# A fused attention and FFN kernel on one core: the room of the DMA scratch given to spare and shifted weight tiles, and the last output block stored in two halves

## Chip, cores and metric

One Trainium2 chip, one core. The metric is device time in microseconds of one launch; three runs of the kernel before gave 801.32, 802.25 and 802.22, median 802.22.

## What is computed

Linear attention with an RMS norm feeds a GELU FFN. All inputs and outputs are float32.

```python
kv = einsum('bhsd,bhse->bhde', k, v)              # 8 batches x 8 heads, seq 576, dim 64
out = einsum('bhsd,bhde->bhse', q, kv)
rms = sqrt(mean(out * out, axis=-1) + 1e-6)
x = (out / rms * g_norm)  -> (4608 tokens, 512)
h = x @ w_in                                      # (512, 2048)
y = 0.5 * h * (1 + erf(h / sqrt(2))) @ w_out      # (2048, 512)
```

## The kernel before

**Precision.** A float32 product is made from three products of halves: each operand is split into hi (rounded to float32r by ScalarE's copy) and lo (what is left, by VectorE's or GpSimd's subtraction), and hi*hi, hi*lo and lo*hi are summed in PSUM. A matmul that uses a lo operand waits for that subtraction.

**Chunks.** The 4608 tokens go in nine chunks of 512. In the loop that begins at line 1109, chunks 0 and 1 compute `layer1` (line 678, twelve matmuls of 512 columns for each of 16 blocks i) and, one block behind, `layer2` (line 705, twelve matmuls with weight tile w_out i as the moving operand). `gelu` writes gh and `rest` (line 697) gl, the lo half that layer 2 needs last.

**Fewer products.** While chunk 1 runs, the kernel makes sums of blocks of the weights, so that from chunk 2 on seven products of quarter blocks do the work of eight. Sums of w_in: `combine` (lines 416 and 433, VectorE), `high_sums` (ScalarE into a staging tile: w_in0 and w_in1, or x2 and x3) and `low_sums` (line 449). Sums of w_out: `sum_out` (line 537, six operations on GpSimd) at the blocks of `EARLY`, then `split_out` one block later (line 1033 on ScalarE, line 1034 on VectorE, twice). The results go to DRAM by SyncE (`product_out`, lines 400 and 405), from where `fetch` (line 500) brings them back into a ring of six SBUF tiles, `RING`; `used` issues the next fetch when a tile's last matmul has been issued. Eleven products don't go through the ring: they are kept in w_out4 to w_out7 (`KEPT_IN`) and in w_out8 to w_out11 and w_in13 to w_in15 (`KEPT_OUT`).

**Layout.** SBUF tiles of 2 x 512 floats a partition are laid out in the order of `PLACES`. `EXTRA` adds floats behind some of them: 64 behind a ring tile, so that a ring tile can be used at its start or 48 floats (`AWAY`) into it; 48 more behind the last ring tile, so that the kept tiles after it begin 48 floats further round than all others; and 16 behind the last kept tile.

**Chunk 2** uses `layer1_pair` for pairs j of blocks and the plain layer 2. `ahead_loads` loads k and v of a later batch, `ahead_matmuls` sums them (`sum_kv`) and projects the next chunk.

**Chunks 3 to 8** (class `Fast`) run layer 1 as `first_part` and `second_part` (line 546, 256 columns) and layer 2 as 28 ticks of twelve matmuls of 256 columns (line 1221). A tick (k, n) is product k for group n of blocks, in the order `TICKS`. `ready(i)` prepares the operand of tick i: hi by ScalarE (line 1198), lo by VectorE (line 1199). `combine(k, n)` (line 1188) adds blocks of the activations in place, which the later ticks read: that for tick 7 reads what `combine(2, 3)` leaves. In a tick the matmuls go in the order hi x wh, hi x wl, lo x wh, so its third matmul is the first that uses lo. `ready` runs `AHEAD` = 4 ticks before its tick, but tick 5 is prepared at the end of layer 1 and tick 6 with the first tick's work. `next_piece` prepares pieces of the next chunk's x between ticks (lines 361 and 366). After four ticks of a product `after` adds its PSUM bank to an earlier sum and stores a 256 x 256 block.

Each engine works through its own queue in the order of the program; SyncE's queue issues nearly all DMAs.

Of the kernel before, what the change touches and what calls it, by code (L numbers as in the profile page):

```python
# [8 lines left out]
F32 = mybir.dt.float32  # L9
# [28 lines left out]
def linear_attn_rms_gelu_ffn(  # L38
# [58 lines left out]
    RINGS = [f"w_in{i}" for i in RING]  # L97
    PLACES = [f"x{i}" for i in range(6)] + [f"w_in{i}" for i in (4, 5, 6, 7, 8, 9, 12)]
    PLACES += [f"w_out{i}" for i in (0, 1, 2, 3, 12, 13, 14, 15)]
    PLACES += RINGS + KEPT_IN + KEPT_OUT  # L100
    EXTRA = {name: 4 * LINE for name in RINGS}
    EXTRA[RINGS[-1]] += AWAY
    EXTRA[KEPT_OUT[-1]] = 4 * LINE - AWAY

# [423 lines left out]
    def keep(key):  # L528
        t = resident[key] = block_tile(KEPT_IN[key[1]], F32R)[:, :2 * DM]
# [543 lines left out]
    EARLY = (6, 8, 10, 12)  # L1073
# [35 lines left out]
    for s in range(PLAIN * NF):  # L1109
# [34 lines left out]
        else:  # L1144
# [17 lines left out]
    class Fast:  # L1162
# [44 lines left out]
        def matmuls(self, i):  # L1207
            k, n = self.ticks[i]
            name = self.BANKS[k]
            if k in (0, 2, 1) and n == 0:  # L1210
                self.bank[name] = bank(name)
            ps = self.bank[name]
            w = operand(self.c, ("out", k, n))
            slot, op = self.ops.pop(i)
            for p in range(2):
                hi, lo = (op[:, z * CH + p * HALF:z * CH + (p + 1) * HALF] for z in range(2))
                wh, wl = (w[:, p * DM + m * HALF:p * DM + (m + 1) * HALF] for m in range(2))
                for a in range(2):
                    at = slice(a * P, (a + 1) * P)
                    for m, (x, y) in enumerate(((hi, wh), (hi, wl), (lo, wh))):  # L1220
                        nc.tensor.matmul(  # L1221
                            out=ps[:, a * HALF:(a + 1) * HALF], lhsT=x[:, at], rhs=y,
                            start=(k in (0, 2, 1) and n + p + a + m == 0),
                            stop=(n == GROUPS - 1 and p == 1 and m == 2), skip_group_check=True,
                        )
            used(self.c, ("out", k, n))
            free.append(slot)

        def after(self, i):
# [6 lines left out]
            name = {0: "gh", 2: "gl", 4: "gl", 6: "gh", 1: "w", 3: "z", 5: "w"}[k]  # L1236
            if name in "zw":
                t = work.tile([P, DM], I32, name=name, bufs=2).bitcast(F32)
            else:
                t = work.tile([P, CH], F32, name=name, bufs=2)  # L1240
            s[k] = t
            if k in (0, 4):
                nc.scalar.copy(out=t, in_=ps)
            else:
                add(t, ps, s[{2: 0, 6: 0, 1: 6, 3: 0, 5: 2}[k]])
# [238 lines left out]
```

## Time and profile before

| | us |
|---|---|
| median of three runs | 802.22 |
| the profiled execution | 801.69 |
| its span | 799.9 |
| TensorE busy (matmul) | 791.7 |
| VectorE busy | 573.3 |
| ScalarE busy | 369.7 |
| GpSimd busy | 210.6 |

The span goes from the first to the last instruction of the profiled execution; about 1.8 us of its time lie around it. In the views, PE is TensorE, DVE VectorE, ACT ScalarE, POOL GpSimd, SP SyncE. A matmul's length in the timeline is modelled and overlaps the next one's, so pace is read from starts and from the chain of waits, whose pieces follow each other without overlap. L1221 is line 1221 of the kernel; tile names are given without their numbers, so w_out4 reads w_out. PEclk, the granted clock as a share of full speed, is 1.00 in all stretches shown.

### The profile page before, as it was taken

The numbers are of one execution on the slowest core, as the hardware profiler recorded it, in microseconds if no ns is written. First come the engines' busy times: TensorE is split into PE (matmuls) and PEld (weight loads), VectorE is DVE, ScalarE is ACT, GpSimd is POOL, SyncE is SP. The second block draws the span as 40 slices with busy tenths as digits, with TensorE's granted clock in tenths as the row PEclk, the third lists the DMA queues.
The fourth block names the chain that finished last, engine by engine and source line by source line (L and its number), as shares of the span: only waits on it lengthen the run. The fifth ranks groups of instructions, "written<-read, shape, count | busy, mean of one in ns | idle before, by whom it ended". The sixth has DMA issues, their size and how long they took to land.

```text
span 799.9 us, 16183 instructions
## 1 busy us (share of the span) xinstructions
PE 791.7 (99%) x6248; PEld 739.4 (92%) x6248; DVE 573.3 (72%) x1029; ACT 369.7 (46%) x702; POOL 210.6 (26%) x184
## 2 busy tenths in 40 slices
PE   9999999999999999999999999999999999999998
PEld 7688888887798889999999999999999999999997
DVE  3999857899647764779376946786579658965683
ACT  2787534454353433446154715463445343632460
POOL 1000021653333503460047002800263026201200
PEclk9999999999999999999999999999999999999999
DMA  9991317999996789999989998989898988899984
GB/s 349 406 375 53 119 28 260 359 350 375 340 357 233 244 323 359 385 353 351 386 298 340 352 358 294 357 308 309 299 327 310 331 302 317 300 316 346 336 296 167
DMA packets 90512, 245.39 MB, mean 307 GB/s; under 512 B 9028, under 2 KB 30788, under 8 KB 90436
## 3 DMA queue, kind: packets, MB, share of 16 engines
q1 hardware_dynamic: 90432, 244.35, 85.2%
q8 instruction: 50, 0.82, 0.4%
q14 instruction: 26, 0.21, 0.1%
q10 hardware_dynamic: 4, 0.00, 0.0%
HBM read 205.52 MB, written 35.13 MB: 301 GB/s over the span
## 4 chain that ended last, share of the span: by engine, by line
PE 88%; DMA 5%; DVE 4%; SPq 1%; issue 1%; ACT 0%; DVEq 0%
PE acc L1221 21%; PE acc L546 17%; PE h L546 15%; PE acc L705 12%; PE a L1221 8%; PE h L678 7%; PE a L242 3%; PE a L181 3%; DMA products_in<-w_in 2%; DMA w_in<-products_in 2%; SPq L405 1%; PE h L670 1%; PE h L790 1%; DVE w L433 1%; DVE z L416 1%
## 5 line engine op out<-in xcount | busy, mean ns | idle before, releaser
L705 PE MATMUL acc<-w_out,gh 128*128 128x512 f32 x312 | 97.8, 394 | 0.0
L229 POOL TENSOR_TENSOR ql<-q,qh 128x512 fp32r<-128x512 f32 x16 | 21.5, 1342 | 262.6 <-ACT qh L228 262.6
L678 PE MATMUL h<-x,w_in 128*128 128x512 f32 x360 | 87.3, 392 | 0.0
L1221 PE MATMUL acc<-w_in,w_out 128*128 128x256 f32 x696 | 86.1, 278 | 0.0
L1221 PEld LDWEIGHTS acc<-w_in,w_out 128*128 128x128 f32 x696 | 82.7, 188 | 0.0
L678 PEld LDWEIGHTS h<-x,w_in 128*128 128x128 f32 x360 | 67.5, 188 | 14.5 <-POOL x L332 0.2
L705 PEld LDWEIGHTS acc<-w_out,gh 128*128 128x128 f32 x312 | 57.9, 188 | 12.4
L705 PE MATMUL acc<-w_out,gl 128*128 128x512 f32 x156 | 61.5, 394 | 1.8 <-DVE gl L697 1.6
L546 PE MATMUL acc<-w_out,w_in 128*128 128x256 f32 x450 | 61.0, 280 | 0.8 <-DMA w_in<-products_in 0.6
L546 PEld LDWEIGHTS acc<-w_out,w_in 128*128 128x128 f32 x450 | 55.6, 188 | 1.4 <-ACT w_out L602 0.8
L691 ACT ACTIVATE gh<-h 128x512 fp32r<-128x512 f32 x39 | 23.2, 595 | 70.1 <-PE h L678 45.9
L546 PE MATMUL h<-w_in,w_in 128*128 128x256 f32 x402 | 52.1, 277 | 0.4 <-DMA w_in<-products_in 0.4
L546 PEld LDWEIGHTS h<-w_in,w_in 128*128 128x128 f32 x402 | 48.7, 188 | 0.7 <-issue 0.5
L546 PE MATMUL acc<-x,w_in 128*128 128x256 f32 x360 | 48.1, 278 | 0.0
L1221 PE MATMUL acc<-w_in,x 128*128 128x256 f32 x360 | 45.5, 278 | 0.0
L546 PEld LDWEIGHTS acc<-x,w_in 128*128 128x128 f32 x360 | 44.3, 188 | 0.2
L1221 PEld LDWEIGHTS acc<-w_in,x 128*128 128x128 f32 x360 | 43.2, 188 | 0.0
L546 PE MATMUL h<-x,w_in 128*128 128x256 f32 x312 | 41.5, 279 | 0.0
L537 DVE TENSOR_TENSOR gl<-acc,gh 128x256 f32<-128x256 f32 (+1 forms) x66 | 29.3, 444 | 16.9 <-ACT gh L583 13.6
L265 DVE TRANSPOSE_TENSOR_REDUCE part<-sq 128x16 f32<-128x512 f32 x33 | 23.4, 709 | 23.1 <-ACT sq L252 23.1
L546 PEld LDWEIGHTS h<-x,w_in 128*128 128x128 f32 x312 | 39.2, 189 | 0.7
L583 ACT COPY gh<-h 128x256 f32<-128x256 f32 x18 | 6.8, 376 | 68.2 <-PE h L546 68.2
(287 smaller groups left out, 1855.9 us busy)
## 6 DMA issues: line engine op xcount, KB each, us to landing
w_in<-products_in SPq DMA_DIRECT2D x172, 512.0 KB, 5.4
w_in<-products_out SPq DMA_DIRECT2D x126, 512.0 KB, 5.4
kv_main<-kv_main SPq DMA_DIRECT2D x22, 512.0 KB, 6.8
products_in<-w_in SPq DMA_DIRECT2D x40, 256.0 KB, 5.3
w_in<-w_in SPq DMA_DIRECT2D x16, 512.0 KB, 10.2
w_out<-w_out SPq DMA_DIRECT2D x16, 512.0 KB, 10.2
q<-qT SPq DMA_DIRECT2D x15, 512.0 KB, 6.7
products_out<-w_out SPq DMA_DIRECT2D x20, 256.0 KB, 4.6
```

The source lines that it names most:

```text
L181: nc.tensor.matmul(out=ps[r, n * D:(n + 1) * D], lhsT=k[:, r], rhs=v[:, r], start=(j == 0), stop=(j == NJ),)
L229: eng.tensor_tensor(out=ql, in0=q, in1=qh.bitcast(F32), op=ALU.subtract)
L242: nc.tensor.matmul(out=ps[:, a:e], lhsT=w, rhs=x[:, a:e], start=(m == 0), stop=(m == 2))
L265: nc.vector.tensor_reduce(out=self.part[:, p, :], in_=sq.rearrange("p (b d) -> p b d", d=BLK), op=ALU.add, axis=AX.X, apply_transpose=True,)
L405: eng.dma_start(out=to.rearrange("p (a n) -> p a n", a=2), in_=src.bitcast(F32))
L416: nc.vector.tensor_tensor(out=whole[a], in0=w[:, HI], in1=w[:, LO], op=ALU.add)
L537: eng.tensor_tensor(out=out, in0=x, in1=y, op=op)
L546: nc.tensor.matmul(out=out, lhsT=y, rhs=x[:, z, kb], start=first and kb + i == 0, stop=kb == 1 and i == 2, skip_group_check=True,)
L678: nc.tensor.matmul(out=h, lhsT=parts["in", i][:, w][:, p * P:(p + 1) * P], rhs=at.x[p][:, x], start=(m + p == 0), stop=(m == 2 and p == NP ...
L691: nc.scalar.activation(out=gh, in_=h, func=AF.Gelu)
L705: nc.tensor.matmul(out=ps, lhsT=x[:, ts], rhs=parts["out", i][:, w], start=(i == 0 and m == 0), stop=(m == 2 and (i == NF - 1 or (i, t) == ...
L1221: nc.tensor.matmul(out=ps[:, a * HALF:(a + 1) * HALF], lhsT=x[:, at], rhs=y, start=(k in (0, 2, 1) and n + p + a + m == 0), stop=(n == GRO ...
```

## The change

The kernel asks for 1 KB of scratch for dynamic DMAs instead of 16, which gives 15 KB a partition to SBUF tiles. There are three new tiles, s0 to s2; every ring tile and every kept tile gets 64 floats behind it, so that all tiles begin at the same residue, and the kept products lie 48 floats into their tiles. s0 and s1 are the staging tiles of `high_sums` for j = 6, s2 one of those of the last `split_out`; later all three join the tiles that `take` gives out. `EARLY` is two blocks earlier. In chunk 2, loads of k and v and their sum move one pair later. In chunk 3 the two calls of `raw_out` move from j = 1 and 3 to 2 and 5. In each of chunks 3 to 8 tick 6 is prepared at the end of layer 1, ahead of the two combines. In the last chunk products 1 and 5 accumulate their two sides in two banks, and the last four ticks run for side 0 first, which is added and stored, and then for side 1.

```diff
-    PLACES += RINGS + KEPT_IN + KEPT_OUT
-    EXTRA = {name: 4 * LINE for name in RINGS}
-    EXTRA[RINGS[-1]] += AWAY
-    EXTRA[KEPT_OUT[-1]] = 4 * LINE - AWAY
+    PLACES += SPARE + RINGS + KEPT_IN + KEPT_OUT
+    EXTRA = {name: 4 * LINE for name in RINGS + KEPT_IN + KEPT_OUT}
...
-                resident[key] = block_tile(KEPT_OUT[KEPT_KEYS.index(key[1])], F32R)
+                t = block_tile(KEPT_OUT[KEPT_KEYS.index(key[1])], F32R)
+                resident[key] = t[:, AWAY:AWAY + 2 * DM]
...
-                t = piece(block_tile(f"x{2 + second}", F32R))
+                t = piece(block_tile(SPARE[second] if j == 6 else f"x{2 + second}", F32R))
...
-        t = resident[key] = block_tile(KEPT_IN[key[1]], F32R)[:, :2 * DM]
+        t = resident[key] = block_tile(KEPT_IN[key[1]], F32R)[:, AWAY:AWAY + 2 * DM]
...
-    EARLY = (6, 8, 10, 12)
+    EARLY = (4, 6, 8, 10)
...
-                split_out(n, [f"w_in{m}" for m in ((4, 5), (6, 7), (4, 5), (6, 9))[n]])
+                split_out(n, (("w_in4", "w_in5"), ("w_in6", "w_in7"), ("w_in4", "w_in5"),
+                              (SPARE[2], "w_in9"))[n])
...
-            if i >= len(self.ticks):
+            if i >= len(self.ticks) or i in self.ops:
                 return
...
-        def matmuls(self, i):
+        def matmuls(self, i, sides=(0, 1)):
...
+            two = self.c == NCH - 1 and name == "a0"
+            if k in (0, 2, 1) and n == 0 and 0 in sides:
+                self.bank[name] = [bank(name), bank("a1")] if two else [bank(name)] * 2
...
-                for a in range(2):
+                for a in sides:
...
-        def after(self, i):
+        def after(self, i, sides=(0, 1)):
...
+            halves = [sides] if ps[0] is ps[1] else [(a,) for a in sides]
+            for part in halves:
+                cols = slice(part[0] * HALF, (part[-1] + 1) * HALF)
+                t, x = s[k][:, cols], ps[part[0]][:, cols]
+                if k in (0, 4):
+                    nc.scalar.copy(out=t, in_=x)
+                else:
+                    add(t, x, s[{2: 0, 6: 0, 1: 6, 3: 0, 5: 2}[k]][:, cols])
...
-            if c + 2 < B and at == (3, 2):
+            if c + 2 < B and at == (4, 2):
                 split_kv(c + 2, range(NP))
...
-        if c + 2 < B and (j, between) == (3, 0):
+        if c + 2 < B and (j, between) == (4, 0):
             sum_kv(c + 2, range(NP))
...
-        if c + 2 < B and j < 2:
-            for p in (2 * j, 2 * j + 1):
-                (load_main if j else load_kv)(c + 2, p)
-        if c + 2 < B and j == 1:
+        if c + 2 < B and 1 <= j < 3:
+            for p in (2 * j - 2, 2 * j - 1):
+                (load_main if j > 1 else load_kv)(c + 2, p)
+        if c + 2 < B and j == 2:
             load_tails(c + 2)
...
-    free += ["x4", "x5", "x0", "x1", "w_in12"]
+    free += ["x4", "x5", "x0", "x1", "w_in12"] + SPARE
...
-            if c == FAST and second and j in (1, 3):
-                raw_out(NJ2 - 2 + j // 2)
-                free.extend(f"w_out{n}" for n in (NF - 5 + j, NF - 4 + j))
+            if c == FAST and second and j in (2, 5):
+                raw_out(NJ2 - 2 + j // 3)
+                free.extend(f"w_out{n + 2 * (j // 3)}" for n in (NF - 4, NF - 3))
...
             if second and j % 2:
-                last = j == NJ2 - 1
                 layer.ready(TICKS.index((0, j // 2)))
+                if last:
+                    layer.ready(TICKS.index((2, j // 2 - 1)))
                 for k in (6, 2):
                     layer.combine(k, j // 2, nc.vector if last else nc.gpsimd)
...
+        if c == NCH - 1:
+            for side in range(2):
+                for i in range(len(layer.ticks) - GROUPS, len(layer.ticks)):
+                    layer.matmuls(i, (side,))
+                    layer.after(i, (side,))
...
-    nc = bacc.Bacc("TRN2", target_bir_lowering=False, num_devices=1)
+    nc = bacc.Bacc("TRN2", target_bir_lowering=False, num_devices=1,
+                   dynamic_dma_scratch_size=1024)
```

How the instructions of an engine stand before and after, at three places. A row is a line, an operation and its tiles with their numbers.

VectorE at the change from layer 1 to layer 2 of chunk 4 (L1199 and L1200 write the lo of a tick's operand, L1188 and L1189 are the combines, L366 and L365 a low block of the next chunk). Before:

```order
L537 TENSOR_TENSOR acc_4982<-acc_4982,gl 128x512
L1199 TENSOR_TENSOR w_out_5094<-x_5042,w_out_5094 128x512
L1188 TENSOR_TENSOR x_5042<-w_in_5043,x_5042 128x512
L1188 TENSOR_TENSOR x_5042<-x_5042 128x512
L1199 TENSOR_TENSOR x_5126<-w_out_4894,x_5126 128x512
L366 TENSOR_TENSOR w_out_5144<-o,w_out_5144 128x512
L1199 TENSOR_TENSOR w_in_5147<-x_5042,w_in_5147 128x512
L1199 TENSOR_TENSOR w_in_5164<-w_in_4550,w_in_5164 128x512
```

Now:

```order
L537 TENSOR_TENSOR acc_4985<-acc_4985,gl 128x512
L1200 TENSOR_TENSOR w_in_5097<-x_5045,w_in_5097 128x512
L1200 TENSOR_TENSOR s_5100<-w_in_4897,s_5100 128x512
L1189 TENSOR_TENSOR x_5045<-w_in_5046,x_5045 128x512
L1189 TENSOR_TENSOR x_5045<-x_5045 128x512
L365 TENSOR_TENSOR w_out_5147<-o,w_out_5147 128x512
L1200 TENSOR_TENSOR w_out_5150<-x_5045,w_out_5150 128x512
L1200 TENSOR_TENSOR x_5167<-w_out_4553,x_5167 128x512
```

The lo of tick 6 (x_5126 before, s_5100 now) went ahead of the two combines; all that follows the combines stands where it stood, the lo of tick 7 among it.

VectorE in chunk 1, around gl of block 13 (L697, h_2135 before, h_2148 now; L356 and L355 add blocks of the next chunk's x, L1034 is `split_out`). Before:

```order
L697 TENSOR_TENSOR gl<-h_2073,gh 128x512
L449 TENSOR_TENSOR w_in_1509<-w,w_in_1509 128x2x256
L356 TENSOR_TENSOR z<-o 128x512
L356 TENSOR_TENSOR o<-o 128x2x256
L356 TENSOR_TENSOR w<-z,o 128x512
L366 TENSOR_TENSOR w_in_2156<-o,w_in_2156 128x512
L697 TENSOR_TENSOR gl<-h_2135,gh 128x512
L1034 TENSOR_TENSOR w_in_2164<-w_in_2116,w_in_2164 128x2x256
L1034 TENSOR_TENSOR w_in_2167<-w_in_2116,w_in_2167 128x2x256
L356 TENSOR_TENSOR z<-o,w 128x512
```

Now:

```order
L697 TENSOR_TENSOR gl<-h_2094,gh 128x512
L449 TENSOR_TENSOR w_in_1512<-w,w_in_1512 128x2x256
L355 TENSOR_TENSOR z<-o 128x512
L355 TENSOR_TENSOR o<-o 128x2x256
L355 TENSOR_TENSOR w<-z,o 128x512
L365 TENSOR_TENSOR w_in_2169<-o,w_in_2169 128x512
L697 TENSOR_TENSOR gl<-h_2148,gh 128x512
L355 TENSOR_TENSOR z<-o,w 128x512
```

The last `split_out` left this place; it now stands two blocks earlier, ahead of gl of block 12, and each of the three others one place of the same kind earlier.

SyncE in layer 1 of chunk 3, from the second send of raw weights (L400) on (L500 is a fetch of the ring, L147 and L164 load k and v; they are L146 and L163 now). Before:

```order
L400 DMA w_in_3511<-w_out_1142 128x2x256
L400 DMA w_in_3513<-w_out_1228 128x2x256
L400 DMA w_in_3515<-w_out_1228 128x2x256
L147 DMA kv_main<-kv_main 128x1024
L164 DMA kv_tail<-kv_tail 128x256
L500 DMA w_in_1500<-products_in_0_2024 128x1024
L500 DMA w_in_1509<-products_in_1_2030 128x1024
L500 DMA w_in_2188<-products_in_2_1900 128x1024
```

Now:

```order
L146 DMA kv_main<-kv_main 128x1024
L163 DMA kv_tail<-kv_tail 128x256
L500 DMA w_in_1503<-products_in_0_2049 128x1024
L500 DMA w_in_1512<-products_in_1_2055 128x1024
L500 DMA w_in_2191<-products_in_2_1921 128x1024
L146 DMA kv_main<-kv_main 128x1024
L163 DMA kv_tail<-kv_tail 128x256
L500 DMA w_in_2193<-products_in_2_2051 128x1024
L500 DMA w_in_2319<-products_out_0_1447 128x1024
L500 DMA w_in_2321<-products_out_1_1602 128x1024
L400 DMA w_in_3602<-w_out_1145 128x2x256
L400 DMA w_in_3604<-w_out_1231 128x2x256
```

The three sends went from ahead of this fetch of products_in_0 to behind the first fetches of products_out.

## Rows read from the trace of the kernel before

**Rows 1.** The page, part 1: busy time, share of the span, instructions.
```profile
PE 791.7 (99%) x6248; PEld 739.4 (92%) x6248; DVE 573.3 (72%) x1029; ACT 369.7 (46%) x702; POOL 210.6 (26%) x184
```

**Rows 2.** The chain that ended last, chunk 0: start us, us, what.
```profile
46.98 2.72 PE acc L705 x12
...
53.38 2.80 PE acc L705 x12
...
94.27 2.80 PE acc L705 x12
```

**Rows 3.** The waits of PE: waited for, us in total, times, longest.
```profile
PE acc L705 <- DVE gl L697: 1.6, 1, 1.6
...
PE acc L546 <- DMA w_in<-products_in: 0.6, 1, 0.6
```

**Rows 4.** The chain, layer 2 of chunks 3 and 4.
```profile
351.37 21.86 PE acc L1221 x192
373.23 5.44 PE a L1221 x48
...
389.55 2.78 PE h L546 x24
...
434.39 22.45 PE acc L1221 x192
456.84 5.65 PE a L1221 x48
...
473.80 2.85 PE h L546 x24
```

**Rows 5.** The timeline of PE, chunk 4, ticks 5 and 6: start us, us, what.
```profile
441.13 1.52 PE L1221 MATMUL acc<-w_in,w_out 128*128 128x256 f32 x12
442.49 1.63 PE L1221 MATMUL acc<-w_in,x 128*128 128x256 f32 x12
```

**Rows 6.** The timeline of DVE at the same place.
```profile
439.99 0.69 DVE L1199 TENSOR_TENSOR w_out<-x,w_out 128x512 fp32r<-128x512 f32 x1 [1.17 <-ACT w_out L1198]
440.60 0.69 DVE L1188 TENSOR_TENSOR x<-w_in,x 128x512 f32<-128x512 f32 x1
441.32 0.69 DVE L1188 TENSOR_TENSOR x<-x 128x512 f32<-128x512 f32 x1
441.93 0.68 DVE L1199 TENSOR_TENSOR x<-w_out,x 128x512 fp32r<-128x512 f32 x1
```

**Rows 7.** The page, part 3: a DMA queue's packets, MB, share of 16 engines.
```profile
q1 hardware_dynamic: 90432, 244.35, 85.2%
```

**Rows 8.** The timeline of DVE, chunk 1, beside the fourth sum of w_out.
```profile
198.15 1.67 DVE L356 TENSOR_TENSOR o<-o 128x512 f32<-128x512 f32 x1
```

**Rows 9.** Windows: PE, PEld, DVE, ACT, POOL busy, PEclk, DMA share, GB/s.
```profile
140.00:150.00 10.00, 10.00 (x48) 8.36 (x47) 7.83 (x12) 5.09 (x10) 5.24 (x4) 1.00 1.05 361
...
190.00:200.00 10.00, 9.87 (x43) 7.76 (x42) 9.86 (x12) 4.78 (x9) 7.39 (x5) 1.00 1.06 365
...
310.00:350.00 40.00, 39.40 (x398) 38.85 (x397) 27.75 (x55) 18.26 (x36) 22.30 (x17) 1.00 1.03 388
```

**Rows 10.** The timeline of SP, chunk 3: the second send of raw weights.
```profile
330.75 1.96 SPq L400 DMA_DIRECT2D w_in<-w_out  x3
```

**Rows 11.** The chain, the fetch that follows it.
```profile
334.90 7.69 DMA w_in<-products_in
```

**Rows 12.** The timeline of ACT, chunk 4: hi of ticks 5 and 7.
```profile
439.35 0.61 ACT L1198 CAST w_out<-x 128x512 fp32r<-128x512 f32 x1
...
442.05 0.62 ACT L1198 CAST w_in<-x 128x512 fp32r<-128x512 f32 x1 [1.05 <-DVE x L1188]
```

**Rows 13.** The chain, its last piece.
```profile
796.08 0.69 DVE w L537
```

**Rows 14.** Line 537 by operation: min/median/max ns, first and last start, forms.
```profile
L537 DVE TENSOR_TENSOR h<-h,gh x18: 399/420/433, 312.9 to 757.3; 128x256 f32<-128x256 f32 x18
```

**Rows 15.** DMA from 793 us on: issues, KB each, median us to landing.
```profile
out<-w SPq DMA_DIRECT2D x1, 256.0 KB, 2.2
```

More of the change, by code (lines that the diff above doesn't have):

```diff
@@ L97, in linear_attn_rms_gelu_ffn @@
     RINGS = [f"w_in{i}" for i in RING]
+    SPARE = ["s0", "s1", "s2"]
     PLACES = [f"x{i}" for i in range(6)] + [f"w_in{i}" for i in (4, 5, 6, 7, 8, 9, 12)]
     PLACES += [f"w_out{i}" for i in (0, 1, 2, 3, 12, 13, 14, 15)]
-    PLACES += RINGS + KEPT_IN + KEPT_OUT
-    EXTRA = {name: 4 * LINE for name in RINGS}
-    EXTRA[RINGS[-1]] += AWAY
-    EXTRA[KEPT_OUT[-1]] = 4 * LINE - AWAY
+    PLACES += SPARE + RINGS + KEPT_IN + KEPT_OUT
+    EXTRA = {name: 4 * LINE for name in RINGS + KEPT_IN + KEPT_OUT}
     def block_tile(name, dtype):
@@ L1205, in linear_attn_rms_gelu_ffn @@
         BANKS = {0: "acc2", 4: "acc2", 2: "acc3", 6: "acc3", 3: "acc3", 1: "a0", 5: "a0"}
-        def matmuls(self, i):
+        def matmuls(self, i, sides=(0, 1)):
             k, n = self.ticks[i]
             name = self.BANKS[k]
-            if k in (0, 2, 1) and n == 0:
-                self.bank[name] = bank(name)
-            ps = self.bank[name]
+            two = self.c == NCH - 1 and name == "a0"
+            if k in (0, 2, 1) and n == 0 and 0 in sides:
+                self.bank[name] = [bank(name), bank("a1")] if two else [bank(name)] * 2
             w = operand(self.c, ("out", k, n))
-            slot, op = self.ops.pop(i)
+            slot, op = self.ops[i]
             for p in range(2):
@@ L1221, in matmuls @@
                         nc.tensor.matmul(
-                            out=ps[:, a * HALF:(a + 1) * HALF], lhsT=x[:, at], rhs=y,
-                            start=(k in (0, 2, 1) and n + p + a + m == 0),
+                            out=self.bank[name][a][:, a * HALF:(a + 1) * HALF],
+                            lhsT=x[:, at], rhs=y,
+                            start=(k in (0, 2, 1) and n + p + m == 0 and (two or a == 0)),
                             stop=(n == GROUPS - 1 and p == 1 and m == 2), skip_group_check=True,
                         )
-            used(self.c, ("out", k, n))
-            free.append(slot)
-        def after(self, i):
+            if 1 in sides:
+                used(self.c, ("out", k, n))
+                free.append(slot)
+                self.ops.pop(i)
+        def after(self, i, sides=(0, 1)):
             k, n = self.ticks[i]
@@ L1235, in after @@
             s = self.sums
[L1236 to L1245, printed above, removed]
+            if 0 in sides:
+                name = {0: "gh", 4: "gl", 2: "gl", 6: "gh", 1: "w", 3: "z", 5: "w"}[k]
+                if name in "zw":
+                    t = work.tile([P, DM], I32, name=name, bufs=2).bitcast(F32)
+                else:
+                    t = work.tile([P, CH], F32, name=name, bufs=2)
+                s[k] = t
+            halves = [sides] if ps[0] is ps[1] else [(a,) for a in sides]
[4 more added lines that the diff above has]
+                    nc.scalar.copy(out=t, in_=x)
+                else:
+                    add(t, x, s[{2: 0, 6: 0, 1: 6, 3: 0, 5: 2}[k]][:, cols])
+            t = s[k][:, sides[0] * HALF:(sides[-1] + 1) * HALF]
             at = {4: (0, 0), 1: (1, 1), 3: (0, 1), 5: (1, 0)}.get(k)
             if at:
-                r = self.c * CH + at[0] * HALF
-                to = out[r:r + HALF, at[1] * HALF:(at[1] + 1) * HALF]
+                r = self.c * CH + at[0] * HALF + sides[0] * P
+                to = out[r:r + len(sides) * P, at[1] * HALF:(at[1] + 1) * HALF]
                 nc.sync.dma_start(
                     out=to.rearrange("(a p) n -> p a n", p=P),
-                    in_=t.rearrange("p (a n) -> p a n", a=2),
+                    in_=t.rearrange("p (a n) -> p a n", a=len(sides)),
                 )
@@ L1425, in linear_attn_rms_gelu_ffn @@
                     layer.ready(i)
+            last = j == NJ2 - 1
             if second and j % 2:
-                last = j == NJ2 - 1
                 layer.ready(TICKS.index((0, j // 2)))
+                if last:
+                    layer.ready(TICKS.index((2, j // 2 - 1)))
                 for k in (6, 2):
@@ L1438, in linear_attn_rms_gelu_ffn @@
                 layer.combine(1, i - 9)
-            layer.matmuls(i)
-            layer.after(i)
+            if c < NCH - 1 or i < len(layer.ticks) - GROUPS:
+                layer.matmuls(i)
+                layer.after(i)
             within_layer2(c, layer, i)
+        if c == NCH - 1:
[3 more added lines that the diff above has]
+                    layer.after(i, (side,))
 def kernel(q, k, v, g_norm, moe_w_in, moe_w_out):
```

## Prediction

> **What bounds the kernel now.** I read the page first. TensorE is busy for 791.7 us, 99% of the span [rows 1]. So an edit counts only where TensorE waits, where its matmuls run slower than elsewhere, or after the last of them. The views behind that: the chain by stretches, because a stretch of equal matmul counts shows by its length where the pace is worse; the waits of TensorE; then the timelines of the engines that feed the place. Three things show.
>
> Pace of 512-column matmuls: in layer 2 of chunk 0 twelve matmuls take 2.72 us with most weight tiles and 2.80 us in the eight rows from 53.38 to 94.27 [rows 2], which are the blocks i = 4 to 11: the tiles w_out4 to w_out11, and by the code those alone begin 48 floats off the others.
>
> Waits: of the longest, 1.6 us stands before a layer-2 block of chunk 1, for VectorE's gl (line 697), and 0.6 us in layer 1 of chunk 3, for a product that the ring fetched [rows 3].
>
> Pace of 256-column matmuls: the first 192 matmuls of layer 2 take 21.86 us in chunk 3 and 22.45 in chunk 4, the next 48 take 5.44 and 5.65, and the next layer 1 begins with 2.78 and 2.85 for 24 [rows 4]. Chunk 5 repeats chunk 4's lengths. Per chunk that is 0.59 + 3 x 0.21 + 0.07 = 1.3 us, and I add an estimated 0.1 for the rest of that layer 1: 1.4 us. It begins at one place. Ticks 5 and 6 start at 441.13 and 442.49, 1.36 us apart; the first is listed with 1.52 us, the second with 1.63 [rows 5]. The third matmul of a tick is the first that needs lo (lines 1220 and 1222); two matmuls into tick 6 is 442.49 + 2 x 1.36/12 = 442.72. VectorE's lo for it (line 1199) runs from 441.93 for 0.68, to 442.61 [rows 6]. So 0.11 us from the end of lo to its matmul is too little, and after this short wait the pace stays slow for the rest of layer 2.
>
> **The change, part by part.**
>
> *Scratch.* Nothing but room is taken. The transfers are on one hardware queue, 244.35 MB [rows 7], which SyncE feeds (ScalarE issues two tiny ones). I cost it at 0; no row tells what a smaller scratch would do to an issue, so the bounds are nothing on one side, and on the other issues that take longer, of which the ring's six tiles hide some tenths of a us each and the last store hides none: 0 to +0.4. [...]
>
> *Residue of the kept tiles.* Eight blocks x 0.08 us in chunk 0: -0.64 [rows 2]. In chunk 1 the same eight stand among VectorE's waits, which can swallow the gain: 0 to -0.64, I take -0.3. In chunk 2 the odd pairs keep gh in w_in13 and w_in14, which lie at the shifted place as well, so that about four of the eight pay now: -0.3. Together -1.2, ends -0.6 and -1.6. That a tile's start sets the pace is a reading of these rows only. [...]
>
> *Sums of w_out two blocks earlier (EARLY).* Before, GpSimd's fourth sum runs beside VectorE's add_blocks from 195.8: an operation of line 356 takes 1.67 us there [rows 8], where the same shape takes 0.69 [rows 6]. VectorE works 9.86 of 10 us from 190 to 200 with GpSimd busy for 7.39, and gl of block 13 comes 1.6 us late [rows 3, 9]. After, this sum stands at block 10, so this stretch is free of it: -1.6. What is paid: all four splits now precede block 12's gl, one more than before: two operations of 128x512, which follow each other by 0.6 us as in [rows 6], so 1.2 us of VectorE, with ScalarE's two copies beside it, and the sums press on earlier operations, about one and a half of them by 1.67 - 0.69 = 0.98, so 1.5 us. VectorE has 10 - 7.83 = 2.2 us to spare from 140 to 150 [rows 9]. The remainder, 1.2 + 1.5 - 2.2 = 0.5, arrives as a wait at block 10, where the first rsqrt and scale stand ahead of gl. Four sends of 256 KB go earlier on SyncE, past the sends of w_in's products; x2 and x3 no longer wait for the staging of j = 6, since it has s0 and s1. Net -1.1; ends -1.6 (all hidden) and +4.0 (see the second rival).
>
> *Chunk 2.* The loads of k and v come one pair later, sum_kv's 40 matmuls and split_kv too. Counts stay, both have pairs of slack, and SyncE's queue in front of its last sends is as before. 0, between -0.6 (its late fetch vanishes) and +0.3.
>
> *raw_out at j = 2 and 5.* Three sends of 256 KB are issued from 330.75 ahead of the fetch of 334.90, which takes 7.69 us to land; at the same time the transfers use a share of 1.03 of the engines [rows 9 to 11]. At 388 GB/s three such sends are 0.79 MB, 2.0 us. Behind the fetch instead of ahead of it, they let it land some 2.0 us sooner, and it was 0.6 late: -0.6 [rows 3]. The later fetches then carry the 2.0 us; they have the ring's depth.
>
> *Tick 6 prepared before the combines.* VectorE's order was lo5, comb6, comb2, lo6, the next chunk's low block, lo7; now it is lo5, lo6, comb6, comb2, low block, lo7. From chunk 4's rows: lo6 takes the start 440.60, 1.33 us sooner, and is no longer late. comb6 then starts at 441.21 (0.61 later), comb2 0.72 after it (441.32 - 440.60), at 441.93 [rows 6]. ScalarE's hi7 reads what comb2 writes: it started at 442.05, 0.73 after comb2 at 441.32 [rows 6, 12], so now at 442.66. lo7 follows its hi by 0.64, as lo5 at 439.99 follows the hi of 439.35 [rows 6, 12], so it starts at 443.30 and ends 0.69 later, at 443.99. Without the wait at tick 6, tick 7 starts at 442.49 + 1.36 = 443.85 and needs lo at 444.08. That leaves 0.09 us, and 0.11 was too little at tick 6. **So the late thing is next lo7**: the same short wait, one tick on, with the same slow pace after it. Chunks 4 and 5 gain one tick of the slow pace, (5.65 - 5.44)/4 = 0.05 us each: -0.1. And chunk 3, whose lo operations were 0.6 us early because TensorE had waited in layer 1, loses that margin with the wait: it then meets the same wait at tick 7 and pays what chunk 4 pays: +1.3. Chunks 6 to 8 run at the fast pace and have no such edge. With raw_out, chunk 3 is +0.7; all of this -0.1 + 0.7 = +0.6.
>
> *Tail.* The last add takes 0.69 us on 128x512 [rows 13]; an add on 128x256 has a median of 0.42 [rows 14]: -0.27. The last store is 256 KB and lands 2.2 us after its issue [rows 15]; half of it saves half of its moving time, an estimated 0.25 us from 128 KB at the 388 GB/s of [rows 9] with a margin for its fixed part. Side 0's add and store lie beside the last 24 matmuls (2.7 us), and the halved add of k = 1 beside the 5.4 us of k = 3. -0.5, ends -0.2 and -0.7.
>
> **Sum.** -1.2 - 1.1 + 0 + 0.6 - 0.5 = -2.2 us. Against the profiled execution (801.69) that is 799.5, against the median of the runs (802.22, 0.53 above it) 800.0; I give 799.8, between them, and count the rivals from the same middle, 802.0.
>
> **The rivals.**
> *The new order is enough* (chance 0.2): lo7 is in time, tick 7 doesn't wait, and chunks 3 to 8 all run at 5.44. For it: 0.09 against 0.11 is a matter of hundredths, and the end of an operation is not exactly where its data are seen. Against: tick 6 failed with more. Time: 2 x 1.4 saved in chunks 4 and 5 and 0.6 in chunk 3, so -1.2 - 1.1 - 0.6 - 2.8 - 0.5 = -6.2, 795.8.
> *Slower: chunk 1 gets a longer wait at block 10 than it loses at block 13* (0.08). The four sends moved ahead are 1.05 MB, 2.9 us at the 361 GB/s of 140 to 150, where the transfers already use 1.05 [rows 9]. If the staging tiles of w_in's sums come free that much later, VectorE can't use its spare 2.2 us, and gl of block 10 is 1.2 + 1.5 + 2.9 = 5.6 us late: 5.6 - 1.6 = +4.0 in place of -1.1, total +2.9, 804.9. It decides from a lateness of 2.7 us (then nothing is gained over before), and can be measured from 4.3. Against it: s0 and s1 free two of these tiles.
> *The residue is not what makes 2.80* (0.1): the eight blocks keep 2.80, because their place in the work sets it and not their address. The term of 1.2 is gone, -2.2 + 1.2 = -1.0, 801.0. Against it: blocks before and after them, in the same work, take 2.72. [...]
>
> **How the numbers follow.** My own case has 0.62 and, from the ends of its terms, 797.6 to 801.6. A measurement of this kernel can tell about 0.2%, 1.6 us, from no change; 800.6 is the edge. Two thirds of my case lie below it (0.41), 0.2 within, 0.01 above. With the first rival (0.20) and a part of the third, faster has 0.63; same 0.27; slower, from the second rival and ends, 0.10. The range reaches down to the first rival and up past the third: 795.4 to 802.6; what is left out is most of the second rival and a few hundredths below.
>
> **What would show it.** Right: eight rows of 2.72 in chunk 0; no wait for gl at block 13 but one of some tenths near block 10; no wait for a fetch in layer 1 of chunk 3; in chunks 3, 4 and 5 the first 192 matmuls near 22.4 and then 5.65; a last add of 0.42 and a store of 128 KB. Wrong: 5.44 in chunks 4 and 5 (lo7 was in time); 5.44 in chunk 3 with its wait in layer 1 still there; rows of 2.80 in chunk 0 (residue); a wait of over 2.7 us in chunk 1.

## The result, and the profile after

| | us |
|---|---|
| kernel before, median of 22 runs | 800.57 (798.35 to 802.30) |
| changed kernel, median of 22 runs | 802.62 (800.78 to 807.02) |
| ratio | 1.0034, 95% interval 1.0022 to 1.0046 |

The change makes the kernel slower: by 0.34%, 2.7 us, as the ratio has it; the medians lie 2.05 us apart, and eight of the changed kernel's 22 runs are longer than 803 us. The forecast was 799.8 us, faster; the measured median lies 0.02 us above the stated range. The forecast counted from 802.0, and the 22 runs of the kernel before give 800.57, so the change itself was missed by more than the times say: 2.2 us gained were forecast, 2.05 to 2.7 were lost. The profiled execution of before (801.69) was a long one among its 22 runs; a second profile of the same kernel, below, shows why.

What was gained stands where it was looked for. The chain that ended last, chunk 0 of the changed kernel (start us, us, what), against [rows 2]:

```profile
46.97 2.72 PE acc L705 x12
...
53.36 2.72 PE acc L705 x12
...
93.61 2.72 PE acc L705 x12
```

All eight rows of 2.80 are 2.72, and chunk 0 is 0.9 us shorter. The rest of the chain, against [rows 4] and [rows 13]:

```profile
214.95 4.83 PE h L546 x42
...
311.85 2.83 PE acc L546 x24
...
353.79 22.09 PE acc L1222 x192
375.87 5.44 PE a L1222 x48
...
437.03 21.95 PE acc L1222 x192
458.99 5.44 PE a L1222 x48
...
520.49 22.41 PE acc L1222 x192
542.90 5.65 PE a L1222 x48
...
797.02 0.43 DVE w L537
```

In the kernel before, the first, second and third of these pieces start at 213.49, 308.82 and 351.37. So chunk 2 starts 1.5 us later although chunk 0 was shorter, chunk 3 starts 3.0 us later, and its layer 1 wins 0.6 back: 41.9 us instead of 42.5. Layer 2 of chunks 3 and 4 runs at 5.44, that of chunk 5 at 5.65. The last add is the short one. The loss is in chunks 1 and 2. The waits of TensorE in the changed kernel (waited for, us in total, times, longest), against [rows 3]:

```profile
PE acc L705 <- DVE gl L697: 4.8, 2, 2.6
PE h L546 <- DVE w_in L537: 1.9, 2, 1.3
```

The wait for gl has grown from 1.6 to 4.8 us, the wait for the ring's fetch is gone, and chunk 2 waits for VectorE's line 537. Windows of chunk 1 (PE, PEld, DVE, ACT, POOL busy, PEclk, DMA share, GB/s), against [rows 9]:

```profile
140.00:150.00 10.00, 10.00 (x48) 8.40 (x47) 9.26 (x14) 5.09 (x10) 5.93 (x5) 1.00 1.03 370
...
180.00:190.00 10.00, 7.43 (x33) 5.78 (x32) 9.62 (x21) 2.35 (x5) 1.39 (x2) 1.00 1.04 385
190.00:200.00 10.00, 7.72 (x34) 6.10 (x33) 9.86 (x13) 5.40 (x11) 4.29 (x3) 1.00 1.06 395
```

VectorE is busy nearly all the time, TensorE is not from 180 to 200. VectorE's timeline there shows where its time goes:

```profile
184.56 0.69 DVE L697 TENSOR_TENSOR gl<-h,gh 128x512 fp32r<-128x512 f32 x1
...
191.84 1.78 DVE L1034 TENSOR_TENSOR s<-w_in,s 128x512 fp32r<-128x512 f32 x1
193.54 1.77 DVE L1034 TENSOR_TENSOR w_in<-w_in,w_in 128x512 fp32r<-128x512 f32 x1
...
198.06 0.68 DVE L697 TENSOR_TENSOR gl<-h,gh 128x512 fp32r<-128x512 f32 x1
```

The first row is gl of block 10, the last gl of block 12. The two operations of the last `split_out`, now ahead of block 12, take 1.78 us each where 0.68 is usual. In between stands GpSimd:

```profile
191.62 1.46 POOL L365 TENSOR_TENSOR x<-o,x 128x512 fp32r<-128x512 f32 x1 [10.23 <-ACT x L360]
193.03 1.74 POOL L228 TENSOR_TENSOR ql<-q,qh 128x512 fp32r<-128x512 f32 x1
```

### The profile page after: what moved, and what is told of

Same layout as the page of the kernel before. It is cut to its first block, busy times and chain, and to the rows that moved or that the text cites. A ratio compares the mean times of both kernels' runs of the same rounds, so it can differ in the third digit from the quotient of the medians.

```text
span 800.1 us, 16160 instructions
## 1 busy us (share of the span) xinstructions
PE 788.6 (99%) x6248; PEld 738.0 (92%) x6248; DVE 577.5 (72%) x1031; ACT 369.8 (46%) x702; POOL 211.9 (26%) x184
## 4 chain that ended last, share of the span: by engine, by line
PE 88%; DVE 5%; DMA 4%; issue 1%; SPq 1%; POOL 0%; ACT 0%; DVEq 0%; POOLq 0%
PE acc L1222 21%; PE acc L546 18%; PE h L546 15%; PE acc L705 12%; PE a L1222 8%; PE h L678 7%; PE a L241 3%; PE a L180 3%; DMA products_in<-x 1%; PE h L670 1%; DMA q<-qT 1%; PE h L790 1%; SPq L405 1%; DMA kv_main<-kv_main 1%; DVE w L433 1%
## 5 line engine op out<-in xcount | busy, mean ns | idle before, releaser
L678 PEld LDWEIGHTS h<-x,w_in 128*128 128x128 f32 x360 | 67.4, 188 | 13.9 <-POOL x L331 0.2
L1222 PE MATMUL acc<-w_in,w_out 128*128 128x256 f32 x456 | 56.9, 277 | 0.0
L546 PE MATMUL h<-w_in,w_in 128*128 128x256 f32 x420 | 54.5, 278 | 1.9 <-DVE w_in L537 1.9
L1222 PEld LDWEIGHTS acc<-w_in,w_out 128*128 128x128 f32 x456 | 54.3, 188 | 0.0
L546 PEld LDWEIGHTS h<-w_in,w_in 128*128 128x128 f32 x420 | 51.0, 188 | 2.5 <-DVE w_in L537 2.5
L1222 PE MATMUL acc<-w_in,w_in 128*128 128x256 f32 x384 | 48.0, 277 | 0.0
L1222 PEld LDWEIGHTS acc<-w_in,w_in 128*128 128x128 f32 x384 | 45.7, 188 | 0.0
L1222 PE MATMUL acc<-w_in,x 128*128 128x256 f32 x336 | 42.7, 277 | 0.0
L546 PE MATMUL acc<-w_in,w_in 128*128 128x256 f32 x300 | 41.6, 278 | 0.0
L705 PEld LDWEIGHTS acc<-w_out,gl 128*128 128x128 f32 x156 | 29.3, 188 | 12.1 <-DVE gl L697 5.9
L1222 PEld LDWEIGHTS acc<-w_in,x 128*128 128x128 f32 x336 | 40.4, 188 | 0.0
L546 PEld LDWEIGHTS acc<-w_in,w_in 128*128 128x128 f32 x300 | 37.6, 188 | 0.2
```

Source lines behind the costliest of these rows:

```text
L546: nc.tensor.matmul(out=out, lhsT=y, rhs=x[:, z, kb], start=first and kb + i == 0, stop=kb == 1 and i == 2, skip_group_check=True,)
L678: nc.tensor.matmul(out=h, lhsT=parts["in", i][:, w][:, p * P:(p + 1) * P], rhs=at.x[p][:, x], start=(m + p == 0), stop=(m == 2 and p == NP ...
L705: nc.tensor.matmul(out=ps, lhsT=x[:, ts], rhs=parts["out", i][:, w], start=(i == 0 and m == 0), stop=(m == 2 and (i == NF - 1 or (i, t) == ...
L1222: nc.tensor.matmul(out=self.bank[name][a][:, a * HALF:(a + 1) * HALF], lhsT=x[:, at], rhs=y, start=(k in (0, 2, 1) and n + p + m == 0 and ...
```

## Experiments

Each run is compared with runs of the kernel before on the same chip; ratios to it are given with their 95% interval. The chips differ (the kernel before has medians from 799.25 to 800.57), so two runs are compared by their ratios. Small differences are read from the chain: where chunk 2 starts, where chunk 3 starts, and the pace of layer 2. Where chunk 2 starts is not exact either: profiles of kernels that are the same up to there differ by 0.1 to 0.6 us, in one case by 1.4. The edits of the first four runs start from the changed kernel.

**EARLY put back.**

```diff
-    EARLY = (4, 6, 8, 10)
+    EARLY = (6, 8, 10, 12)
```

(with the four places of `split_out` as before).

> The changed kernel with EARLY and the places of split_out put back as before; s0 and s1 still serve the staging of j = 6. [...] Theory B (TensorE reaches block 10 about 0.9 us sooner since the weights' residue no longer slows it, and VectorE would be late anyway): a wait of 0.7 us or more stays at block 10, and blocks 12 and 13 wait longer than before by what block 10 does not take, so that less than 2 us is gained.

Measured: 802.08 us, ratio 1.0020 (1.0010 to 1.0029); chunk 2 starts at 214.19. B's size holds, under 2 us, but its place does not: block 10 waits only 0.3 us, and the waits for gl are still 3.5 us, most of it now at block 12. The ratio is 0.14% below the changed kernel's 1.0034, 1.1 us, and the intervals overlap; chunk 2 starts 0.8 us sooner. So the earlier sums are at most a part of the loss, and something else holds VectorE ahead of block 12. VectorE in this run, the two operations of `split_out`, and GpSimd beside them:

```profile
189.63 3.47 DVE L1034 TENSOR_TENSOR w_in<-w_in,w_in 128x512 fp32r<-128x512 f32 x2
```

```profile
189.41 1.45 POOL L365 TENSOR_TENSOR x<-o,x 128x512 fp32r<-128x512 f32 x1 [10.23 <-ACT x L360]
190.82 1.74 POOL L228 TENSOR_TENSOR ql<-q,qh 128x512 fp32r<-128x512 f32 x1
192.52 3.41 POOL L537 TENSOR_TENSOR w_in<-w_out 128x512 f32<-128x512 f32 x2
```

In the kernel before, GpSimd's same three began 3.1 to 3.3 us later and met nothing of `split_out`; ScalarE's copy into x2, on which the first depends, had waited for a DMA (its timeline and GpSimd's, kernel before):

```profile
191.84 0.62 ACT L361 CAST x<-o 128x512 fp32r<-128x512 f32 x1 [2.29 <-DMA products_in<-x]
```

```profile
192.54 1.62 POOL L366 TENSOR_TENSOR x<-o,x 128x512 fp32r<-128x512 f32 x1 [12.62 <-DMA products_in<-w_in]
...
195.82 3.44 POOL L537 TENSOR_TENSOR w_in<-w_out 128x512 f32<-128x512 f32 x2
```

That DMA reads the staging tile x2, which s0 now replaces.

**Chunk 2's loads put back.**

```diff
-        if c + 2 < B and 1 <= j < 3:
-            for p in (2 * j - 2, 2 * j - 1):
-                (load_main if j > 1 else load_kv)(c + 2, p)
-        if c + 2 < B and j == 2:
+        if c + 2 < B and j < 2:
+            for p in (2 * j, 2 * j + 1):
+                (load_main if j else load_kv)(c + 2, p)
+        if c + 2 < B and j == 1:
```

(with `split_kv` at (3, 2) and `sum_kv` at (3, 0)).

> The changed kernel with chunk 2's loads of k and v at j = 0 and 1 again, and their sum and split at j = 3. Theory C (the load of q at j = 2 now stands behind two loads and the tails on SyncE, lands 7.1 us after its issue, and by ScalarE, GpSimd's low half and GpSimd's scale holds VectorE, so that TensorE waits 1.3 us at 261): the waits for VectorE's line 537 in chunk 2 fall from 1.9 us to under 0.7, chunk 2 is 1.2 to 1.6 us shorter, and the run is as much faster than the changed kernel; chunk 1 is unchanged. Rival D (the waits in chunk 2 come from chunk 1's lateness, from its sends that still fill the queue): no difference.

Measured: 801.12 us, ratio 1.0012 (1.0002 to 1.0023), 0.22% or 1.8 us below the changed kernel's; its list of waits has none for line 537 any more, chunk 1 ends as in the changed kernel (chunk 2 starts at 214.77), and chunk 2 takes 95.1 us instead of 96.9. C holds. The chain of the changed kernel had shown the way:

```profile
243.32 7.11 DMA q<-qT
...
250.46 0.63 ACT qh L227
...
251.16 1.29 POOL ql L228
...
255.59 1.30 POOL o L314
...
260.75 0.44 DVE w_in L537
```

**Both put back.**

> Both put back. [...] By B and D under 2 us faster than the changed kernel, and no faster than before.

Measured: 800.28 us, ratio 1.0002 (0.9991 to 1.0014). By the ratios this is 2.6 us below the changed kernel, and the two alone gave 1.1 and 1.8: they roughly add, to more than the 2 us that B and D allow, and EARLY's part is the smaller. The kernel is level with the one before and not faster.

**Both put back, the first combine ahead of tick 5's operand.**

```diff
-                layer.ready(TICKS.index((0, j // 2)))
                 if last:
+                    layer.combine(6, j // 2)
+                    layer.ready(TICKS.index((0, j // 2)))
+                    layer.combine(2, j // 2)
                     layer.ready(TICKS.index((2, j // 2 - 1)))
-                for k in (6, 2):
-                    layer.combine(k, j // 2, nc.vector if last else nc.gpsimd)
+                else:
+                    layer.ready(TICKS.index((0, j // 2)))
+                    for k in (6, 2):
+                        layer.combine(k, j // 2, nc.gpsimd)
```

> Both put back, and at the end of layer 1 of chunks 3 to 8 the first combine goes ahead of the operand of tick 5, the second between those of ticks 5 and 6. By the timeline of the kernel before, the first combine then runs from about 439.5, lo5 from 440.1, the second combine from 440.7, lo6 from 441.3, hi7 from 441.4 and lo7 from at most 442.5: every lo ends 0.6 us or more ahead of its matmul. If the short wait at tick 7 starts the slow pace in a part of the executions (seen in chunk 5 here, not in 3 and 4), all six chunks run at 5.44 us for 48 matmuls and this run is 0.4 to 3 us faster than the one with both put back. If the slow pace has another cause, 5.65 is seen again in some chunk.

Measured: 798.81 us, ratio 0.9987 (0.9977 to 0.9997), 1.5 us less than the run before it. Layer 2 takes 21.86 and 5.44 us in every chunk:

```profile
352.10 21.86 PE acc L1221 x192
373.96 5.44 PE a L1221 x48
...
435.12 21.86 PE acc L1221 x192
456.99 5.44 PE a L1221 x48
...
518.49 21.86 PE acc L1221 x192
540.35 5.44 PE a L1221 x48
```

The run with both put back had 5.65 in chunk 3.

This profile shows one thing more. TensorE waits 2.9 us for gl of block 12, until 196.84, and soon after it begins again its granted clock falls from 1.00 to 0.50. Windows (PE, PEld, DVE, ACT, POOL busy, PEclk, DMA share, GB/s):

```profile
195.00:196.00 1.00, 0.00 (x0) 0.00 (x0) 0.96 (x2) 0.00 (x0) 0.92 (x2) 1.00 1.04 393
...
198.00:199.00 1.00, 1.00 (x3) 0.79 (x3) 0.96 (x2) 0.87 (x2) 1.00 (x1) 0.50 1.06 260
...
202.00:203.00 1.00, 1.00 (x6) 0.83 (x5) 1.00 (x2) 0.47 (x1) 0.45 (x1) 1.00 0.27 102
```

There three matmuls take 1.28 us instead of 0.69. Block 13's gl matmuls begin 7.2 us after block 12's; in the run with only EARLY put back, where the clock stays at 1.00 after a like wait, it is 5.8 without the wait between them. So this wait cost some 1.4 us more than its length, and chunk 2 starts 0.4 to 0.6 us later here than in the runs with EARLY or both put back, which are the same up to there. Two other profiles show the fall too, after 2.4 and 2.6 us (chunk 2's loads put back, and EARLY alone, below); the changed kernel's own does not. Each run also has its mean granted clock on record. It is 0.998 or less in 49 of 75 runs of the six kernels whose longest wait for gl in the profile is 2.4 to 2.9 us, and in none of 100 runs of the kernels whose longest is 1.6 or less. Of the changed kernel's 22 runs it is so in 14, with a median of 803.5 us against 802.0 for the other eight. What makes the clock fall in one execution and not in the next stays open.

**The staging put back**, on top of that.

```diff
-                t = piece(block_tile(SPARE[second] if j == 6 else f"x{2 + second}", F32R))
+                t = piece(block_tile(f"x{2 + second}", F32R))
```

> The kernel with EARLY and chunk 2's loads put back and the combine first, and now also the staging of j = 6 in x2 and x3 again instead of s0 and s1. Theory S (in the kernel before, ScalarE's copy into x2 waited 2.3 us for the DMA that reads x2, and so GpSimd's low half of x, its low half of q and the fourth sum began 3.1 us later, at 192.5; without that wait they run beside VectorE's two operations of split_out, which then take 3.47 us instead of 1.29, and gl of block 12 comes late): the two operations take about 1.3 us again, GpSimd's low half of x begins 2 to 3 us later, the wait at block 12 falls from 3 to under 2 us, and chunk 2 begins 0.5 to 1.5 us sooner than in the run with s0 and s1. Rival R (TensorE simply comes 1.5 us sooner to a VectorE that is never idle): the waits for gl stay at 3 us or more in sum, and chunk 2 begins within 0.3 us of 213.9.

Measured: 796.34 us, ratio 0.9956 (0.9943 to 0.9970); against 0.9987 without this edit that is 0.3%, 2.5 us, and the intervals do not overlap. Chunk 2 starts at 212.39, against 214.62. Three profiles without this edit that are alike up to there have 214.01 to 214.62, three with it (two of them below) 212.26 to 212.51: 1.5 to 2.4 us. VectorE's and GpSimd's timelines, with this edit:

```profile
189.30 1.29 DVE L1034 TENSOR_TENSOR w_in<-w_in,w_in 128x512 fp32r<-128x512 f32 x2
```

```profile
191.79 1.30 POOL L365 TENSOR_TENSOR x<-o,x 128x512 fp32r<-128x512 f32 x1 [12.94 <-ACT x L360]
...
194.74 3.44 POOL L537 TENSOR_TENSOR w_in<-w_out 128x512 f32<-128x512 f32 x2
```

And without it, the run before:

```profile
189.34 3.47 DVE L1034 TENSOR_TENSOR w_in<-w_in,w_in 128x512 fp32r<-128x512 f32 x2
```

```profile
189.12 1.45 POOL L365 TENSOR_TENSOR x<-o,x 128x512 fp32r<-128x512 f32 x1 [10.23 <-ACT x L360]
```

So the edit moves GpSimd by 2.7 us, VectorE's two operations are back at 1.29 us, and TensorE's wait at block 12 falls from 2.9 to 0.4 us; 1.6 us stand at block 13 again, as in the kernel before. All five runs have a granted clock of 1.00, so what the fall of the clock cost is in the 2.5 us too. S holds; R falls. This kernel beats both.

**The fourth sum of w_out in chunk 2**, on top of that.

```diff
-    EARLY = (6, 8, 10, 12)
+    EARLY = (6, 8, 10)
-    SUMS = {1: (4,), 3: (5,), 5: (6,), 7: (7,)}
+    SUMS = {1: (4,), 2: (3,), 3: (5,), 5: (6,), 7: (7,)}
```

> The same, and the fourth sum of w_out is made in chunk 2, at j = 2, instead of at block 12 of chunk 1, its split at j = 3. By theories S and R alike, 8 us of GpSimd and two operations of VectorE leave the stretch in which VectorE is never idle: the wait at block 13 goes and the one at block 12 shrinks by the 0.5 us or so that the scale operations lose beside the sum; chunk 2 begins 1 to 2 us sooner. If chunk 2 has room, the whole is 1 to 2 us faster than the run before it; if VectorE's line 537 or a late fetch waits for it there, less.

Measured: 795.70 us, ratio 0.9959 (0.9946 to 0.9971), not to be told from the run before it. Chunk 2 starts 2.4 us sooner (209.99), and takes 1.8 us longer: line 537 is 0.9 us late once more, and a fetch 0.9. Ahead of line 537 stands GpSimd's scale at 252. The sum itself was done by then; the scale waits for VectorE's transpose (line 318), and ahead of that VectorE now has the sum's split, 1.3 us at 250.

**The residue alone**, on the kernel before: the smaller scratch, `EXTRA` and the two slices at `AWAY` of the change, nothing else.

> The kernel before, with the smaller scratch and all tiles at one residue, the kept products 48 floats into their tiles, and nothing else. If the residue makes 2.80 of 2.72, the eight rows of chunk 0 read 2.72 and chunk 0 ends 0.8 us sooner. If chunk 1 is bound by VectorE, the wait for gl grows by what TensorE gains, so that chunk 2 begins less than 0.4 us sooner than at 213.3; if not, 1.3 us sooner. In chunk 2 and 3 the wait for the fetch stays. The run is 0 to 1 us faster than the kernel before.

Measured: 798.59 us, ratio 0.9991 (0.9982 to 1.0000). Chunk 0 reads 2.72 in all rows, and chunk 2 starts at 213.06, 0.3 to 0.4 us sooner; the waits for gl grow to 2.5 us. Chunk 2 takes 95.7 us, where the two profiles of the kernel before have 95.3 and 95.5, with a wait of 0.8 us for a fetch: nothing is gained there. So VectorE swallows most of what layer 2 gains in chunk 1.

**The kernel before, a second profile.**

> The kernel before, a second profile. The slow pace after the wait at tick 6 came in both of its chunks 4 and 5 there, but after the like wait at tick 7 in only 4 of 12 chunks of the changed kernels. If it is a matter of chance, this profile has it in none or one of the two and its span is 1.4 or 2.8 us shorter than 799.9; if the old order makes it, 5.65 us stand in both again.

Measured: 799.09 us, a span of 797.2. The same instructions in the same order:

```profile
434.48 21.97 PE acc L1221 x192
456.45 5.44 PE a L1221 x48
...
517.96 21.97 PE acc L1221 x192
539.93 5.44 PE a L1221 x48
```

The short wait at tick 6 is still in the 21.97 (21.86 without it), but the slow pace isn't: tick 6 of chunk 4 takes 1.47 us here and 1.46 in the first profile, and the ticks after it 1.36 here and 1.41 to 1.42 there. Over all profiles with a short wait at tick 6 or 7, 5.65 follows it in 6 of 19 chunks; in the seven runs with the combine first, in none of 21.

Against this profile the changed kernel's 2.9 us can be followed through the chain: chunk 2 starts 1.6 us later and takes 1.4 us longer, layer 1 of chunk 3 is 0.7 us shorter, layer 2 of chunk 3 to layer 1 of chunk 6 takes 1.3 us more (the slow pace in chunk 5), and the end is 0.7 us shorter.

**EARLY alone**: the run with the staging put back, and the earlier sums with s2.

> The run with the staging put back, and EARLY at 4 to 10 again, with s2 for the last split: the earlier sums without the staging in s0 and s1. Theory A2 (one more split and one more sum ahead of block 10, where VectorE has no idle time, cost by themselves): a wait of 2 to 3 us at block 10 comes back, the wait at block 13 goes, chunk 2 begins 1 to 2 us later than 212.2, and the run is 1 to 2 us slower than with EARLY put back. Rival S2 (it was the staging alone that made the sums collide): no wait over 1 us at block 10, chunk 2 begins at 212.2 or sooner, and the run is as fast or faster.

Measured: 797.52 us, ratio 0.9965 (0.9951 to 0.9979). One wait of 2.6 us in the list, at block 10, none at 12 or 13; chunk 2 starts at 213.49, 1.1 us later than without. A2 holds in its place and at the low end of its size; the ratios alone (0.9965 and 0.9956) overlap. In this profile the granted clock falls to 0.50 after the wait, so the 1.1 us hold that too.

**The fourth sum at j = 4 of chunk 2.**

> The run with the fourth sum of w_out in chunk 2, the sum at j = 4 instead of 2, so that GpSimd's scale of the next chunk at j = 3 no longer stands behind it. If the scale behind the sum made the wait of 0.9 us for line 537 at 258, that wait goes and the gain of 2.4 us up to the start of chunk 2 is kept but for the wait for the fetch near 281 (0.9 us): chunk 3 begins near 305.5 to 306, against 307.0 and 307.6, and the run takes 794 to 795 us. If chunk 2 loses elsewhere what chunk 1 gains, it stays at 795.5 or more.

Measured: 796.67 us, ratio 0.9955 (0.9941 to 0.9970). Missed: two waits for line 537 instead of one, 2.3 us in all. The wait at 258 did go, since the split no longer stands ahead of the scale; but the sum now runs beside add_blocks, and its split stands in VectorE's queue ahead of the chunk's own additions. Chunk 2 starts at 211.43, 1.4 us later than in the run with the sum at j = 2, though the two are the same up to there: one of VectorE's operations (line 314) ahead of block 12 takes 1.76 us beside GpSimd here and 0.69 there.

**The tail put back**, and **raw_out put back**, each on the run with the staging put back.

> The run with the staging put back, and the last output block stored whole as in the kernel before. By the profiles, from the start of the last matmul to the end of the span it takes 4.1 us before and 3.4 in the changed kernel: 0.5 to 0.8 us slower with the whole block, all of it after the last matmul. If the tail is bound by the fixed part of a store, under 0.3.

> The run with the staging put back, and raw_out at j = 1 and 3 of chunk 3 again. If the two sends ahead of the fetch made the wait there, layer 1 of chunk 3 takes 42.5 us again instead of 41.9, and the run is 0.5 to 0.7 us slower. If the wait went for another reason (chunk 2's sends, the spare tiles), it stays at 41.9.

Measured: tail, 797.43 us, ratio 0.9962 (0.9948 to 0.9976); the last add starts at 790.99 and the span ends at 794.8, 3.8 us later; with the halves it is 791.42 and 794.5, 3.1. The halves are worth 0.7 us. raw_out, 797.31 us, ratio 0.9961 (0.9946 to 0.9977): the chain shows the fetch again, as in [rows 11], and layer 1 of chunk 3 takes 42.4 instead of 41.9 us:

```profile
335.06 6.95 DMA w_in<-products_in
```

Both ratios overlap with 0.9956; these two results rest on the profiles. With the residue alone, raw_out unmoved, layer 1 of chunk 3 took 41.9 us too: that wait is a matter of some tenths. TensorE reached chunk 3 at 308.8 with the residue alone and in the kernel before alike, so what decides it is not shown.

## Why the prediction was wrong

- **Residue, right in its cause, wrong in what it is worth.** The eight rows went to 2.72. But I took chunk 0's 0.64 us as gained, chunk 1's as half swallowed and 0.3 for chunk 2. A wait further on takes what was gained ahead of it as well: alone, the residue brought 0.3 to 0.4 us to the start of chunk 2, and nothing in chunk 2, in place of 1.2.
- **Staging in s0 and s1, the step that failed.** The prediction said that x2 and x3 "no longer wait" and costed that at nothing. It cost about 2 us, 2.5 by the ratios (0.9987 against 0.9956) and 1.5 to 2.4 at the start of chunk 2, measured with the sums at their old blocks; no other part cost clearly more. The wait removed was ScalarE's, 2.3 us for a DMA, off the path; it had kept GpSimd's work 3 us away from VectorE's `split_out`, and ahead of block 12 VectorE sets the end. A part of the price that no term had is the clock: after a wait of this length its granted level was 0.50 for some 3 us in three profiles of six.
- **EARLY, wrong in sign.** The forecast was a wait of 0.5 us at block 10 and 1.1 us gained; measured, a wait of 2.6 us there (in the changed kernel and in EARLY alone), and 0.8 to 1.1 us lost at the start of chunk 2. By the ratios the loss is as large, but not clear of the noise. The wait at block 13 did go. Two things were too low: GpSimd's first sum met VectorE's line 433, which took 1.15 and 1.51 us in the changed kernel (0.38 and 0.42 with EARLY put back), and TensorE, sped up by the residue, came to block 10 sooner, which the terms counted as a gain elsewhere and not as lateness here. The second rival had the place and the kind of loss, with 0.08, but another cause: no staging tile made VectorE idle; it was busy for 9.6 us and more of each 10 from 150 to 200.
- **Chunk 2, costed at 0, was 1.4 to 1.8 us** (96.9 us, against 95.1 with the loads put back and 95.3 and 95.5 in the kernel before). "Pairs of slack" was said of k and v themselves. What was late is the load of q behind them on SyncE, and by it four engines' work in a row. Its bounds, -0.6 and +0.3, left out the transfer queued behind the moved ones.
- **Ticks 6 and 7, right in place, wrong in price.** The wait moved to tick 7, and chunk 3 has it too. VectorE's lo7 and TensorE's ticks 7 and 8 in chunk 4 of the changed kernel:

```profile
445.94 0.69 DVE L1200 TENSOR_TENSOR w_out<-x,w_out 128x512 fp32r<-128x512 f32 x1
```

```profile
446.49 1.62 PE L1222 MATMUL acc<-w_out,w_out 128*128 128x256 f32 x12
447.94 2.32 PE L1222 MATMUL acc<-w_in,x 128*128 128x256 f32 x19
```

  lo7 ends at 446.63, two matmuls into the tick is 446.72: 0.09 us, as worked out, and the tick takes 1.45 us instead of 1.36. In chunk 3 it takes 1.59, in chunk 5 1.48. But the slow pace, which I took as its sure price (1.3 us a chunk), follows only sometimes: in one chunk of three here, chunk 5. The two slow chunks of the first profile of before were a draw that the second did not repeat, and the sum was made from them.
- **raw_out** -0.6 was right here, and 0.4 to 0.5 in the run that puts it back. **Tail** -0.5, measured -0.7.

Left unsettled: what decides whether the slow pace follows the short wait. The runs show only that it didn't come without the wait (none of 21 chunks, against 6 of 19 with it), and that the wait's length does not decide it (0.10 us in the first profile of before, 0.11 in the second). Unsettled too is why the longest runs of the changed kernel take up to 807.02 us; none of them was profiled.

## What to carry to other kernels

A wait that is off the path can be what keeps two engines apart (here ScalarE's 2.3 us, whose removal cost about 2 us): before a staging tile or buffer is added, look at what the waiting engine will run sooner, and beside whom. Where one engine has no idle time, count every edit as work added to or taken from that engine, and take speed gained ahead of it as lateness there (the residue alone brought 0.3 to 0.4 us to the start of chunk 2, of 1.2 forecast). When loads move on a queue, look at the load behind them: here that of q came late, 7.1 us on the chain, at a price of 1.8 us by the ratios. A long wait of TensorE can cost more than its length (some 1.4 us more after the 2.9 us in the run with the combine first), so the granted clock behind it is worth a look. A single profile can hold a costly chance event (the slow pace of chunks 4 and 5, 1.3 us each); a second profile of the same kernel tells a mechanism from a draw.

## What the runs showed of the hardware

Twelve matmuls of 512 columns take 2.80 us with the moving tile 48 floats off the others and 2.72 with all tiles at one residue: eight rows each in the kernel before and in the residue alone.

A VectorE subtraction of 128x512 with two inputs in SBUF (line 1034) took 0.68 us alone (changed kernel, from 153.77) and 1.78 beside GpSimd's subtractions (from 191.84); two of them took 1.29 and 3.47 us. VectorE's transposes (line 318), with one input, took 0.70 and 0.71 us beside GpSimd's line 537 (192.74 and 194.55 in the run with the combine first, where that line's two operations take 3.41 us from 192.23). In two runs it was the engine that started second that took long: with the fourth sum at j = 2 of chunk 2, VectorE's line 314 starts at 190.77 and takes 0.69, and GpSimd's subtraction starts at 190.85 and takes 1.77; with the sum at j = 4, GpSimd's starts at 191.09 and takes 1.29, and VectorE's at 191.17 takes 1.76.

A wait of 0.10 us ahead of a matmul (tick 6, chunk 4, first profile of before) was followed by the pace of 5.65 instead of 5.44 us for 48 matmuls of 256 columns over the rest of layer 2, some 250 matmuls; a wait of 0.11 us at the same place in the second profile was not. The granted clock was 1.00 in both.

After waits of 2.4 to 2.9 us TensorE's granted clock fell to 0.50 in three profiles, for some 3 us in each, and stayed at 1.00 after such waits in three others.
